# One more pair of batch 2 in cluster order: seven pairs instead of six, with the scatters and waits around it moved

## The chip, the cores and the metric

One core of a Trainium2 chip runs the whole program. The metric is the device time of one execution in microseconds; lower is better. The time before is the median of three runs, 943.9 us (943.89 to 946.26).

## The reference

q, k and v have shape (4, 8, 768, 64): 4 batches, 8 heads, 768 tokens of 64 numbers. Every query and every key is assigned to the one of 16 centroids of its head that it is most similar to, and a query sees only keys of its own cluster:

```python
q_assign = np.argmax(np.einsum('bhsd,hcd->bhsc', q_n, c_n), axis=-1)
k_assign = np.argmax(np.einsum('bhsd,hcd->bhsc', k_n, c_n), axis=-1)
mask = q_assign[:, :, :, None] == k_assign[:, :, None, :]
scores = np.where(mask, scale * np.matmul(q, k.transpose(0, 1, 3, 2)), -1e9)
attn = softmax(scores)                      # over the keys
x = np.matmul(attn, v)                      # -> (4 * 768, 512), heads side by side
h = x @ w_in                                # 512 -> 2048
g = np.maximum(h, 0.0) + alpha * np.minimum(h, 0.0)
return g @ w_out                            # 2048 -> 512
```

## The kernel before, in words

Two heads form a pair, so there are 16 pairs; pairs 0 to 3 belong to batch 0, 4 to 7 to batch 1, 8 to 11 to batch 2 and 12 to 15 to batch 3. The feed-forward network (FFN) of a batch follows its attention and is cut into two halves of 384 tokens.

**Dense pairs.** Attention of a pair is computed in two halves of 384 queries. For each half there are six chunks of 128 keys: `score` (L762) multiplies 384 queries by 128 keys for each of the two heads (L781), ScalarE exponentiates (L799, L802) into one of the E tiles (named E and more), VectorE multiplies by the mask (L822, `mask`), adds the chunks up (L832), turns the sum (L870) and reduces it (L878). TensorE folds that to the denominators (`total`, L891), VectorE takes reciprocals (`invert`, L904) and spreads them (L911); `weigh` multiplies E by v (L936), and `normalise` writes the outcome to the FFN's input xT (L1039).

**Near pairs.** From pair NO = 10 on, the tokens of a pair are first put in the order of their clusters. Then the keys of one chunk can only meet the queries of a `window` (L741) around it: 224, 384, 320, 320, 384 and 224 queries instead of twice 384. Both halves are done in one pass of three steps (`weigh_near`, L956, L969; `normalise_near`, L972, L975). What this costs:
- Ordering: `load` of q and k, `order_features` (two transposes on VectorE, L565), `order_sims` (L573), an argmax (L402 to L410), a transpose (L582) and a scan over the tokens (L587), `order_begins` (two products on TensorE, L599), `order_ranks` and `order_rows` (L607 to L620), `order_clusters` (L637 to L643). The list ORDERS (L1366) holds the step at which each near pair's load is issued; its features follow one step later.
- Scattering: `order_stage` (L652) loads 256 tokens of one head of q, k and v into one of two stage buffers with three DMAs of the SP queue (L659); `order_scatter` (L664) sends 64 tokens of q with 64 of k and v, each to the place that its rank (the tile off) says, by an indirect DMA that GpSimd issues (L673). A pair takes six stages and 24 scatters. They wait in the deque `sorting`; the main loop (L1561 to L1567) takes one per slot, two in the slots of a stage's first step, and none where the pair of the stage before is near. Each such slot begins with `pace` (L646): ScalarE copies one number and GpSimd copies that copy (L649, L650), through one of eight buffers, so that GpSimd doesn't run ahead of the program.
- Loading in order: `order_load` (L679) reads the scattered rows back: the tokens' own numbers into the tile found, q and k in blocks (L694) and v (L703), all on SP. `order_blocks` (L710) and `order_queries` (L716) transpose them on VectorE, one step before the pair's first step.
- Putting back: `to_rows` (L999) transposes the outcomes on TensorE, three tiles at a time and twice; `put_back` (L1005) issues twelve indirect DMAs on GpSimd (L1008), each behind a pace; `fetch_back` (L1013) reads the rows (L1020, SP) and `turn_back` writes them to xT (L1027, VectorE).

**The order of the work** is written out by hand. `steps` (L725) lists the steps: three to a half of a dense pair, three to a near pair. I call three such steps a stage and name it by its first step. In batch 2 the near pairs 10 and 11 come first (steps 48 to 53), then the first halves of pairs 8 and 9 (54 to 59), then their second halves (60 to 65); batch 3 has four near pairs (66 to 77). Each step has five slots (two are taken by the scores in a stage's first step). `begun_at` divides the steps into blocks; at the start of a block `feed_block` (L1423) appends the pieces of one FFN half to the deque `ffn`, and the slots of the block take them at an even rate: 16 pieces `hidden` (L1063, TensorE; L1069 copies, ScalarE; L1055 slopes, VectorE) and 12 pieces `final` (L1081; L1087 or L1089 adds up y). `kept` (L1432) says how many pieces a block leaves to the next one: 12 at the end, 8 before batch 3, 2 at step 60. `later(slots, piece)` (L95) runs a piece some ticks later; a stage has 15 ticks. `prep_at` and `load_at` (L1367 to L1410) place the preparation of each pair by its first step u: features and blocks of q and k (L364), `prep_sims` (L381), `prep_clusters` (L442), keys (L457), and the loads.

The last FFN halves, batch 3's, run in a form with fewer products (`last_pieces`, L1139; L1241 and L1297), with sums formed on VectorE (L1126, L1137, L1220, L1229). Its hidden pieces p1, p5, p2, p6, p3, p7 and the late p4 share banks of PSUM: p4 writes the bank that p7's plus reads.

`check_inverses` (L335) reduces the reciprocals of a batch to their lowest and highest (L340); `inverse` (L329) calls it when the first reciprocal of the next batch is due. The tail (L1579 to L1636) forms a flag from such numbers that says whether a general path has to run; on the inputs here it doesn't.

[...]

## Time and profile before

| | |
|---|---|
| median of three runs | 943.9 us |
| the profiled execution | 944.23 us |
| its span, first to last instruction | 942.5 us |
| TensorE (PE) busy | 924.1 us |
| VectorE (DVE) busy | 663.5 us |
| GpSimd (POOL) busy | 351.2 us |
| ScalarE (ACT) busy | 265.9 us |
| granted TensorE clock | 0.999 |
| scatters (L673), 144 | 1079 ns each |
| returns (L1008), 72 | 1040 ns each |

The page gives busy time by engine and in 40 slices of 23.6 us each, where a digit is the busy share in tenths. Lines of waits read "engine line waited for: us in total, times, longest us". A line of the timeline gives the start, the length of a run of equal instructions, engine, source line, operation, tiles and shape, and how many; an idle stretch ahead of it stands in brackets. A matrix product of 32-bit numbers appears as two records. The table of windows gives busy us of each engine in a stretch:

```profile
core 0: us, PE busy (x) PEld busy (x) DVE busy (x) ACT busy (x) POOL busy (x), PEclk, DMA share, GB/s
445.50:470.10 24.60, 24.60 (x113) 13.43 (x112) 21.50 (x43) 7.47 (x26) 10.77 (x18) 1.00 0.91 151
470.10:508.20 38.10, 36.01 (x151) 17.54 (x150) 29.16 (x59) 7.92 (x22) 14.81 (x25) 1.00 0.22 42
508.20:532.00 23.80, 22.22 (x111) 13.01 (x110) 20.93 (x39) 8.77 (x27) 14.23 (x22) 1.00 0.18 38
532.00:562.30 30.30, 30.30 (x108) 14.65 (x108) 21.07 (x36) 8.28 (x30) 23.93 (x37) 1.00 0.22 55
```

These four stretches are the stages 48, 51, 54 and 57 of the kernel before: near pairs 10 and 11, and the first halves of pairs 8 and 9.

### The profile page before, as it was taken

Reading aid. Unit: us, or ns where it says so; the run is one execution under the profiler, and the core shown is the slowest. Engines: PE = TensorE matmul, PEld = TensorE weight load, DVE = VectorE, ACT = ScalarE, POOL = GpSimd, SP = SyncE. Lnnn points to the kernel's source line nnn. Section 1 sums busy time; section 2 is a strip of 40 time slices with the busy share of each in tenths; the row PEclk is TensorE's granted clock in tenths of the full one; section 3 lists DMA queues with packets and bytes.
Section 4 is the critical chain, followed back from the end, with each engine's and each line's share of the span. In section 5 each row is a group of like instructions: output and inputs, shape, how many; then the busy total and the mean of one; then the engine's idle time right before and its main releaser. Section 6 shows DMA issues by size and latency. Waiting matters only on the chain.

```text
span 942.5 us, 11891 instructions
## 1 busy us (share of the span) xinstructions
PE 924.1 (98%) x3995; PEld 496.5 (53%) x3995; DVE 663.5 (70%) x1247; ACT 265.9 (28%) x658; POOL 351.2 (37%) x529
## 2 busy tenths in 40 slices
PE   8999999999999999999999999999999999999997
PEld 5534444445455454454544545545455555556886
DVE  5797788799679589698995955456888535698100
ACT  5764444323123032331322322223133121221000
POOL 2333222200016576467534686364256670000000
PEclk9999999999999999999999999999999999999999
DMA  8333658039001645165920134333441112000000
GB/s 297 125 127 96 146 130 149 18 59 198 1 6 53 159 87 133 47 120 131 155 52 12 43 80 101 63 67 62 93 75 34 32 37 53 1 0 1 23 23 26
DMA packets 209668, 73.38 MB, mean 78 GB/s; under 512 B 194288, under 2 KB 198080, under 8 KB 209600
## 3 DMA queue, kind: packets, MB, share of 16 engines
q1 hardware_dynamic: 201840, 60.35, 29.2%
q0 software_dynamic: 6912, 11.81, 4.1%
q8 instruction: 33, 0.54, 0.2%
q10 hardware_dynamic: 848, 0.39, 0.2%
q14 instruction: 35, 0.29, 0.1%
HBM read 49.89 MB, written 22.28 MB: 77 GB/s over the span
## 4 chain that ended last, share of the span: by engine, by line
PE 87%; DVE 6%; SPq 2%; DMA 2%; issue 1%; POOL 1%; ACT 1%; ACTq 0%; DVEq 0%; POOLq 0%
PE fps L1081 26%; PE fps L1063 25%; PE vps L936 7%; PE sps L781 7%; PE sps L1297 4%; PE sps L1241 4%; PE fps L781 2%; PE vps L1297 2%; PE vps L1241 2%; PE fps L1297 1%; PE fps L1241 1%; PE sps L790 1%; PE vps L969 1%; PE mps L969 1%; PE mps L381 1%
## 5 line engine op out<-in xcount | busy, mean ns | idle before, releaser
L1063 PE MATMUL fps<-xT,w_in_sb 128*128 128x384 f32 x768 | 257.7, 490 | 0.0
L1081 PE MATMUL fps<-w_out_sb,gT 128*128 128x512 f32 x576 | 254.4, 595 | 1.1 <-DVE gT L1055 1.1
L1063 PEld LDWEIGHTS fps<-xT,w_in_sb 128*128 128x128 f32 x768 | 142.8, 190 | 102.6 <-issue 3.8
L1081 PEld LDWEIGHTS fps<-w_out_sb,gT 128*128 128x128 f32 x576 | 107.5, 190 | 133.4 <-issue 123.0
L673 POOL DMA_INDIRECT scratch<-stage,off x144 | 155.4, 1079 | 49.7 <-issue 25.1
L650 POOL COPY paced<-pace 1x1 f32<-1x1 f32 x196 | 55.5, 283 | 202.3 <-ACT pace L649 201.5
L1069 ACT COPY gT<-fps 128x384 f32<-128x384 f32 x96 | 46.0, 479 | 215.6 <-PE fps L1063 215.6
L1055 DVE SCALAR_TENSOR_TENSOR gT<-gT,alpha 128x384 f32<-128x384 f32 x96 | 61.3, 648 | 50.4 <-ACT gT L1069 50.3
L781 PE MATMUL sps<-qkT 64*128 64x384 f32 (+1 forms) x480 | 88.6, 487 | 0.0
L1008 POOL DMA_INDIRECT back<-rows,found x72 | 74.9, 1040 | 18.2 <-issue 16.1
L802 ACT ACTIVATE E<-sps 128x768 f32<-128x768 f32 (+1 forms) x78 | 57.9, 790 | 59.4 <-PE sps L790 38.8
L781 PEld LDWEIGHTS sps<-qkT 64*128 64x128 f32 x480 | 42.7, 186 | 40.5 <-issue 15.0
L822 DVE SCALAR_TENSOR_TENSOR more<-aq,key,more 128x384 f32<-128x384 bf16 (+2 forms) x120 | 63.0, 584 | 1.2 <-ACT more L799 1.1
L936 PE MATMUL vps<-E,vt 128*64 128x384 f32 x316 | 58.6, 495 | 1.4 <-DVE xT L1039 1.4
L904 DVE RECIPROCAL inverses<-mps 64x12 f32<-64x12 f32 (+1 forms) x44 | 10.9, 248 | 58.5 <-PE mps L891 58.1
L822 DVE SCALAR_TENSOR_TENSOR E<-aq,key,E 128x384 f32<-128x384 bf16 (+2 forms) x96 | 50.2, 577 | 1.9 <-ACT E L799 1.8
L271 POOL TENSOR_TENSOR w_in_sb<-w_in_sb,power 128x512 f32<-128x512 f32 x16 | 25.1, 1573 | 67.8 <-DVE w_in_sb L268 67.8
L832 DVE TENSOR_TENSOR acc<-acc,E 128x768 f32<-128x768 f32 x37 | 35.3, 953 | 14.7 <-ACT E L802 13.6
L271 POOL TENSOR_TENSOR w_out_sb<-w_out_sb,power 128x512 f32<-128x512 f32 x16 | 22.9, 1434 | 57.3 <-DVE w_out_sb L268 57.3
L802 ACT ACTIVATE more<-sps 128x768 f32<-128x768 f32 (+1 forms) x42 | 31.1, 775 | 33.1 <-PE sps L781 32.0
L1087 ACT COPY y<-fps 128x512 f32<-128x512 f32 x18 | 10.6, 586 | 99.1 <-PE fps L1081 99.1
L1089 DVE TENSOR_TENSOR y<-y,fps 128x512 f32<-128x512 f32 x24 | 16.4, 683 | 29.1 <-PE fps L1081 29.1
(283 smaller groups left out, 1167.2 us busy)
## 6 DMA issues: line engine op xcount, KB each, us to landing
raw<-in_moe_w_in_dram SPq DMA_DIRECT2D x16, 512.0 KB
raw<-in_moe_w_out_dram SPq DMA_DIRECT2D x16, 512.0 KB
out_dram<-y SPq DMA_DIRECT2D x21, 256.0 KB
qk<-in_q_dram SPq DMA_DIRECT2D x48, 96.0 KB
qk<-in_k_dram SPq DMA_DIRECT2D x48, 96.0 KB
qk<-scratch SPq DMA_DIRECT2D x48, 96.0 KB
w_in_kept<-w_in_sb SPq DMA_DIRECT2D x8, 512.0 KB
vt<-in_v_dram SPq DMA_DIRECT2D x10, 384.0 KB
```

The source lines that it names most:

```text
L650: nc.gpsimd.tensor_copy(out=sorts["paced"], in_=token)
L673: nc.gpsimd.indirect_dma_start(out=scratch[n][1][h * NX + xx], out_offset=bass.IndirectOffsetOnAxis(ap=ranks[n][:, xx, h:h + 1], axis=0), ...
L781: nc.tensor.matmul(out=bank(ps, h, m), lhsT=qkT[r:r + D, S + c * P:S + (c + 1) * P], rhs=qkT[r:r + D, tokens], start=True, stop=not early_ ...
L802: nc.scalar.activation(out=E[:, :, 0:m], in_=ps[:, :, 0:m], func=AF.Exp, scale=SCALE)
L822: nc.vector.scalar_tensor_tensor(out=e, in0=of, scalar=keys[n][:, NJ + c, h:h + 1], in1=e, op0=ALU.is_equal, op1=ALU.mult)
L936: nc.tensor.matmul(out=po[r:r + D, 0:HS], lhsT=vts[n][:, h, c, :], rhs=e[:, h, :], start=(c == 0), stop=(c == NJ - 1))
L1008: nc.gpsimd.indirect_dma_start(out=to[i], out_offset=bass.IndirectOffsetOnAxis(ap=place[:, h, j:j + 1], axis=0), in_=rows[j // HJ][:, j % ...
L1055: nc.vector.scalar_tensor_tensor(out=gs[f], in0=gs[f], scalar=alpha[:, f:f + 1], in1=gs[f], op0=ALU.mult, op1=ALU.max)
L1063: nc.tensor.matmul(out=ps[:, 0:HS], lhsT=w_in_sb[:, c, f * P:(f + 1) * P], rhs=xTs[b, half][:, c, :], start=(c == 0), stop=(c == NCH - 1))
L1081: nc.tensor.matmul(out=ps[:, 0:DM], lhsT=gs[f][:, i * P:(i + 1) * P], rhs=w_out_sb[:, f, :], start=on and f == f0, stop=off and f == f0 + ...
L1241: nc.tensor.matmul(out=bank[to], lhsT=w_in_form(m, x, cc), rhs=rhs[:, cc, :], start=start and cc == 0, stop=cc == KH - 1, skip_group_check ...
L1297: nc.tensor.matmul(out=bank[to], lhsT=g_form(m, x, t), rhs=w_out_form(n, x), start=start and x == 0, stop=x == NQ - 1, skip_group_check=no ...
```

## The change

- NO becomes 9, so pair 9 is near too: seven pairs are ordered, scattered, computed in one pass and put back. ORDERS has seven entries; the last two loads move from one at step 50 to steps 56 and 59.
- Batch 2 now has the near pairs 9, 10 and 11 (steps 48 to 56) and the two halves of pair 8 (57 to 62), in one block; batch 3 begins at step 63 and the loop ends at step 75 instead of 78. Batch 2's FFN halves are both appended at step 63. The blocks that end at 48 and 63 keep two pieces each.
- `scatters_at` says how many scatters a slot may issue: up to step 50 one more in the first slot of a stage's second and third step (16 in three steps instead of 14), none in steps 51 to 56, one in some slots of 57 to 59 (8), and 20 in three steps from 60 on.
- `order_load` comes three steps ahead of the pair instead of four for pairs 11 and 15 too, and puts the tokens' numbers into the tile off, which held the ranks, instead of a tile found.
- `check_inverses` runs three ticks behind the last reciprocal of a batch instead of ahead of the first of the next; `turn_back` comes seven ticks behind `fetch_back` instead of nine; `prep_blocks` and `prep_sims` move by a slot in some steps; in the last FFN, slopes(f1) moves behind p7's plus, and the pieces are interleaved with the tail's small operations.

```diff
@@ -102,7 +102,7 @@
 
 
     pairs = [(b, hp) for b in range(B) for hp in range(NCH)]
-    NO = WHOLE * NCH - 2
+    NO = WHOLE * NCH - 3
     NP = len(pairs)
     raw_qk, vts = {}, {}
 
@@ -324,12 +324,14 @@
     lowest = const.tile([P, B], FP32, name="lowest")
     highest = const.tile([P, B], FP32, name="highest")
     WORDS = [float((127 + e) * 2 ** 23) for e in (-50, 40)]
-    kept_of = [0]
+    kept_of, inverted = [0], [0] * B
 
     def inverse(n, half):
 
-        if pairs[n][0] > kept_of[0]:
-            check_inverses()
+        b = pairs[n][0]
+        inverted[b] += 1
+        if inverted[b] == 2 * NCH and b < B - 1:
+            later(3, check_inverses)
         return inverses[:, (2 * n + half) % (2 * NCH), :]
 
     def check_inverses():
@@ -679,7 +681,8 @@
     def order_load(n):
         assert len(scattered[n]) == 2 * NX
         whole = scratch.pop(n)[0]
-        found = sorts["order"].tile([P, 2, NJ, 1], I32, name="found")
+        found = ranks[n].rearrange("p x h -> p (x h)")[:, 0:2 * NJ].rearrange(
+            "p (h j d) -> p h j d", h=2, d=1)
         for h in range(2):
             r0 = 2 * h * S
             nc.sync.dma_start(out=found[:, h], in_=whole.bitcast(I32)[
@@ -729,10 +732,10 @@
         begun_at.append(len(steps))
         steps += [(n, None, s) for n in whole for s in range(SB)]
         for half in range(2) if rest else ():
-            if half:
+            if half and not whole:
                 begun_at.append(len(steps))
             steps += [(n, half, s) for n in rest for s in range(SB)]
-            feeds[len(steps)] = b, half
+            feeds[len(steps)] = [(b, 0), (b, 1)] if whole else [(b, half)]
     begun_at.append(len(steps))
     assert NJ == 6 and GROUP == 2
 
@@ -1026,7 +1029,7 @@
             for half in range(2):
                 nc.vector.transpose(out=x_tile(b, half)[:, hp, :],
                                     in_=raw[:, half * HS:(half + 1) * HS])
-        later(4 if n == NP - 1 else 9, turn_back)
+        later(4 if n == NP - 1 else 7, turn_back)
 
     def x_tile(b, half):
         if (b, half) not in xTs:
@@ -1267,10 +1270,10 @@
 
             def p3():
                 plus(g_of(f1, 1), product("e", "S4", x_of(1, 1), False))
-                slopes(f1)
 
             def p7():
                 plus(g_of(f2, 1), product("a", "S3", x_of(1, 0), False))
+                slopes(f1)
                 late.append(p4)
                 if x % 2 == 0 and x:
                     g_sums(x - 2)
@@ -1363,7 +1366,7 @@
     FREE = SLOTS * SB - 3
 
 
-    ORDERS = [26, 29, 35, 38, 41, 50]
+    ORDERS = [26, 29, 35, 38, 41, 56, 59]
     prep_at, load_at = {}, {}
     for (n, half), u in start_of.items():
         def at(step, slot, piece):
@@ -1374,7 +1377,7 @@
             for i in range(2):
                 at(t + 1, FIRST + i, lambda n=n, i=i: order_features(n, i))
             at(t + 2, 2, lambda n=n: order_sims(n))
-            load_at.setdefault(u - (3 if n == NO + 1 else 4), []).append(
+            load_at.setdefault(u - (3 if n in (NO + 1, NO + 2, NP - 1) else 4), []).append(
                 lambda n=n: order_load(n))
             at(u - 4, 0, lambda n=n: prep_clusters(n))
             for i in range(2):
@@ -1395,9 +1398,11 @@
                     at(u - 4, FIRST + g, lambda n=n, g=g: prep_features(n, g))
             else:
                 for w in range(2):
-                    at(u - 7, FIRST + w, lambda n=n, w=w: prep_blocks(n, w))
+                    at(u - 7, FIRST + w + (u - 7 == TOGETHER - 1),
+                       lambda n=n, w=w: prep_blocks(n, w))
             at(u - (3 if n < NCH else 5 if u - 6 < TOGETHER else 6), FIRST,
-               lambda n=n: prep_sims(n))
+               lambda n=n: prep_sims(n)) if u - 6 < 2 * TOGETHER else at(
+                   u - 6, FIRST + 1, lambda n=n: prep_sims(n))
             if n >= NCH:
                 at(u - 4, FIRST if u - 4 < TOGETHER else 0, lambda n=n: prep_clusters(n))
         if n < NCH:
@@ -1412,6 +1417,17 @@
     KEEP = 2
     ffn = deque()
 
+    def scatters_at(v, s, i):
+
+
+        if v < SB:
+            return 1 + (s == 0 or i == 0)
+        if v < 3 * SB:
+            return 0
+        if v < 4 * SB:
+            return int(s == 0 or i % 2 == 0)
+        return 1 + (s == 0 or i % 2 == 0)
+
     def feed(pieces):
         for _ in range(pieces):
             ffn.popleft()()
@@ -1427,12 +1443,13 @@
                 ffn[i] = lambda piece=ffn[i], p=p: (piece(), w_in_sums(p))
             ffn.extend(last_pieces())
             return
-        ffn.extend(ffn_pieces(*feeds[u]))
+        for b, half in feeds[u]:
+            ffn.extend(ffn_pieces(b, half))
 
     def kept(u):
 
 
-        return {NS: 12, begun_at[-2]: 8, begun_at[-3]: 2}.get(block_end(u), 0)
+        return {NS: 12, begun_at[-2]: 2, begun_at[-3]: 2}.get(block_end(u), 0)
 
     def block_end(u):
         return min(x for x in begun_at if x > u)
@@ -1558,7 +1575,7 @@
             places = (block_end(u) - block_start(u)) // SB * FREE
             pieces = len(ffn) - kept(u) + -whole * (places - 1 - at_slot) // places
             todo.popleft()()
-            room = 0 if steps[u - SB][1] is None else 1 + (s == 0)
+            room = scatters_at(u - start_of[NO, None], s, i)
             if room and sorting:
                 pace()
             while sorting and room:
@@ -1577,14 +1594,17 @@
             tick()
         feed(1)
     sum_x(slice(0, 4))
+    feed(2)
     good = const.tile([P, 2], FP32, name="good")
     check_inverses()
+    feed(1)
     nc.vector.tensor_reduce(out=good[:, 0:1], in_=highest, axis=AX.X, op=ALU.max)
     nc.vector.tensor_reduce(out=good[:, 1:2], in_=lowest, axis=AX.X, op=ALU.min)
     nc.vector.tensor_scalar(out=good[:, 0:1], in0=good[:, 0:1], scalar1=WORDS[1],
                             scalar2=None, op0=ALU.is_le)
     nc.vector.tensor_scalar(out=good[:, 1:2], in0=good[:, 1:2], scalar1=WORDS[0],
                             scalar2=good[:, 0:1], op0=ALU.is_ge, op1=ALU.mult)
+    feed(1)
     nc.vector.tensor_reduce(out=good[:, 0:1], in_=alpha, axis=AX.X, op=ALU.max)
     nc.vector.tensor_scalar(out=good[:, 1:2], in0=good[:, 0:1], scalar1=1.0,
                             scalar2=good[:, 1:2], op0=ALU.is_le, op1=ALU.mult)
@@ -1595,7 +1615,7 @@
     for i, p0 in enumerate((P // 2, P // 2 + 1, 0, 1)):
         nc.tensor.matmul(out=ps[0:m, i * NN:(i + 1) * NN], lhsT=ident[:, p0:p0 + m],
                          rhs=sorts["begins"], start=True, stop=True)
-    feed(1)
+    feed(2)
     nc.vector.tensor_copy(out=spans.rearrange("p i n -> p (i n)"), in_=ps[0:m, 0:4 * NN])
     last = const.tile([m, 2], FP32, name="last")
     nc.vector.tensor_tensor(out=last[:, 0:1], in0=ident[0:m, NC - 1:NC],
@@ -1609,6 +1629,7 @@
                                 scalar1=last[:, 0:1], scalar2=last[:, 1:2],
                                 op0=ALU.mult, op1=ALU.add)
 
+    feed(2)
     tiles = const.tile([m, 2, NN], I32, name="tiles")
     nc.vector.tensor_copy(out=tiles[:, 0, :], in_=spans[:, 0, :])
     nc.vector.tensor_scalar(out=tiles[:, 1, :], in0=spans[:, 1, :], scalar1=-1.0,
```

## The prediction

> **What bounds the kernel now.** I read the share of busy time first, then the 40 slices, then what TensorE waited for, and last the timeline of one dense and one near stage. (A stage is three steps, one pair or one pair and half.)
>
> ```profile
> PE 924.1 (98%) x3995; PEld 496.5 (53%) x3995; DVE 663.5 (70%) x1247; ACT 265.9 (28%) x658; POOL 351.2 (37%) x529
> ...
> PE   8999999999999999999999999999999999999997
> ...
> DVE  5797788799679589698995955456888535698100
> ```
>
> TensorE is full in every slice but the first and the last, so work taken from it shortens the kernel one for one, as long as no other engine becomes late. VectorE is the engine to watch: 9 in the slices around 400 to 500 us.
>
> ```profile
> PE mps L599 <- DVE simT L587: 1.6, 1, 1.6
> PE mps L381 <- DVE qk L975: 1.2, 1, 1.2
> ...
> PE mps L969 <- DVE inverses L904: 0.9, 1, 0.9
> ```
>
> These waits (us, times, longest) lie at 516, 478 and 474 us: with 0.9 us late at L1241 and a few before 200 us they are all that TensorE loses after the first 100 us. All three come where VectorE is late, in batch 2's near stages.
>
> ```profile
> 605.59 1.56 PE L781 MATMUL sps<-qkT 64*128 64x384 f32 x8
> ...
> 607.73 0.40 PE L891 MATMUL mps<-part,fold 128*128 128x24 f32 x2
> 608.06 3.45 PE L936 MATMUL vps<-more,vt 128*64 128x384 f32 x20
> ...
> 612.08 0.92 PE L781 MATMUL fps<-qkT 64*128 64x384 f32 x4
> ...
> 614.21 1.12 PE L1081 MATMUL fps<-w_out_sb,gT 128*128 128x512 f32 x2
> ```
>
> One dense half of pair 9, in batch 2: differences of starts give 2.14 us of scores, 0.33 of sums, 4.02 of weighing, 2.13 of scores: 8.62 us.
>
> ```profile
> 696.36 1.29 PE L781 MATMUL sps<-qkT 64*128 64x224 f32 x8
> ...
> 698.12 0.42 PE L891 MATMUL mps<-parts,fold 128*128 128x48 f32 x2
> 698.47 1.79 PE L969 MATMUL vps<-more,vt 128*64 128x384 f32 x16
> ...
> 701.76 0.81 PE L781 MATMUL fps<-qkT 64*128 64x320 f32 x4
> ...
> 703.52 5.43 PE L1063 MATMUL fps<-xT,w_in_sb 128*128 128x384 f32 x16
> 708.78 0.49 PE L999 MATMUL mps<-ident,qk 128*128 128x128 f32 x3
> 709.11 1.13 PE L1063 MATMUL fps<-xT,w_in_sb 128*128 128x384 f32 x3
> ```
>
> A whole near pair: 1.76 + 0.35 + 3.29 + 1.76 = 7.16 us, and 0.33 us for each three transposes of its outcomes.
>
> **What the Trainium skill says.** "Perfetto Trace Analysis", Tensor Engine Instruction: the end of a matmul is estimated by the profiler, so I use starts. The trace agrees that ends mislead: L1063 has a mean of 490 ns, but starts 323 ns apart. "TensorEngine Tiling (Array Packing)", Key Properties: different tiles of the array run in parallel. The trace agrees: eight records of 64 rows (two heads) take 1.39 us to the next group, eight L1063 records of 128 rows 2.6 us; hence I price attention by its own rows, not by columns. "DMA: Bandwidth & Descriptors", SWDGE vs HWDGE: descriptors of DMAs issued by GpSimd are made in software on it, so each scatter costs POOL time (here 1.08 us, against some 0.6 us of SP for one of its DMAs). "VectorE: DVE Perf Modes", The DRAIN you can't avoid: the next operation does not start before the pipe is empty. Here it starts 50 to 90 ns before the end shown of the one ahead; stage 51 (474.13 to 499.85, no idle) took 25.7 us where its mean durations add to 28.5. So I multiply sums of VectorE durations by 0.90.
>
> **The change, part by part.**
>
> 1. Pair 9 from two dense halves to one near pass. TensorE loses 2 x 8.62 = 17.24 us and gets 7.16 + 2 x 0.33 + 0.47 (its order_begins, four records as at 393.03) = 8.29 us. L381 gives way to L573, eight records each. Net 9.0 us off TensorE, all of it on the bound engine: **-9.0**.
>
> 2. VectorE gets less too. Dense pair 9: 24 masks x 0.607, ten adds x 0.951, two turns and two sums (3.8), 4 recip (0.9), two spreads (1.14), two products (1.1), prep 1.9, four query transposes (2.3), argmax 2.6, keys 0.5: about 38.5. Near: masks 6.3, adds 3.5, turns and sums 3.8, recip and spreads 1.8, products 1.1, turn_back 1.1, L710 and L716 3.8, keys 0.5, ordering 11: about 33. The total is no danger; where it lies is.
>
> 3. The stages of batch 2. I added the program's instructions in their new order, at these rows' durations, from one denominator (L891, L904) to the next; VectorE already times 0.90:
> - 42: TensorE 23.2, VectorE 27.0 (one FFN piece went to the next stage, and two are kept); 45: 30.8 and 25.6
> - 48, 51, 54 (near 9, 10, 11): TensorE 23.1, 29.1, 22.3; VectorE 21.5, 24.7, 17.0
> - 57, 60 (pair 8's halves): TensorE 25.4, 28.9; VectorE 25.7, 31.1. In 60 VectorE does 12 masks 7.3, five adds 4.8, ranks of 14 4.6, features and argmax of 15 5.6, blocks and queries of 12 3.8, slopes and y 3.3 and some 5 more: 34.5 before the factor.
> - batch 3: TensorE about 43 a stage, since both halves of batch 2's FFN lie there; VectorE 19 to 27.
> Before, the batch 3 stages were 25 to 28 us and batch 2's last two 43 and 38. So the filler moves behind the stages in which VectorE is loaded. What TensorE needs early: sums (L878) come 5 to 6 us ahead of VectorE's last instruction, and are in time in 45, 60 and 63. L599 needs the scan (L587), near the head of VectorE's stage: in 45 it comes 0.6 us late (4.2 + 5.6 against 9.2), in 60 on time, in 63 about 2 us late (VectorE enters some 3 us behind: 31.1 + 0.5 + 0.5 - 28.9; 3 + 5.1 against 6.3). Cost **+2.6**; zero to six as ends.
>
> 4. Waits that go: check_inverses out of the path of invert (0.9 at 474; the two L340, 0.25 us each, now run behind masks), prep_sims a slot later (1.2 at 478), pair 15's order off step 51 (1.6 at 516). Each of those near stages now has VectorE ahead by 1.6 to 5 us, so nothing else is late in their place: **-3.7**, or 0 if a neighbour takes their place.
>
> 5. slopes(f1) behind p7's plus: TensorE waits 0.9 us once for VectorE, at 860; p4 still waits for that plus. 0; at most -0.9. The interleaved feeds of the tail: TensorE has no wait between 700 and 860 to remove; 0, since the 12 kept pieces (36 us) still cover the return of pair 15, whose L1027 ends at 786 while TensorE asks at 789.5 for it. If that cover goes, each us is lost; its POOL work hangs on the same start, so it doesn't.
>
> 6. found in off's place: its load waited for all scatters anyway; 0 (both bounds a few 0.1 us). turn_back two ticks (3 to 4 us) earlier: the fetches were issued at 523.6 and their packets ended near 528.5, VectorE came at 533.6; VectorE waits 0 to 2 us in stage 54, which has 5 spare; 0.
>
> 7. POOL and SP. 24 scatters and 12 returns more: 24 x 1.08 + 12 x 1.04 + 6 x 0.29 + 9 x 0.28 = 43 us on an engine at 37%; ACT's nine pace copies, 1.7 us of 28%. Per stage of batch 1: 16 x 1.08 + 12 x 0.28 + 4 x 0.29 = 21.8 of 23 to 36 us. Worst is 57 and 60: 12 returns and 8 scatters (27.4 of 25.4), then 6 and 20 with 18 paces and five stage copies (34.3 of 28.9): POOL ends 7 to 8 us late and makes it up in 63 (26.4 of 43). Behind it on SP stand the order loads: pair 13 needs its last scatter at (61, 0), loads at 62, is used at 65; pair 15 (68, 0), 69, 71. A load took 446.8 to about 457, 10 us; so 13 has about 29 us spare, 15 about 18. SP also waits at 59 for the tile of pair 15's raw load, until about 25 us into stage 57; landed 3.5 us into 60, wanted at 6. Eight pace buffers stand for some 16 us before ACT would wait. Cost 0; the other end is a rival.
>
> Sum against the profiled execution (944.2 us, span 942.5): -9.0 + 2.6 - 3.7 = -10.1, so 934.1; the median of the runs is 0.3 below it: **934.0**.
>
> **Rivals.**
> - VectorE takes half back. If in 57 to 63 the overlap is smaller (factor 1: 63.1 us against 54.3) TensorE waits about 4.5 us more than reckoned for L599, L710 and the sums, and the waits of part 4 go on: 944.2 - 9.0 + 4.5, about 939.5. For it: 19.7 of 20 us busy at 460 to 500. Against it: the 25.7 us measured.
> - No change (941 to 946.7): the FFN pieces are too few in batch 2 and waits of about 9 us spread over 42 to 63; or the return of pair 15 (6.6 us of VectorE waiting for that DMA) becomes the end. About 943.
> - Slower: SP's reloads of the two stage buffers stop overlapping with scatters. Exposed, a reload round is 4.3 us of scatters, 2.2 to land, 1.9 of SP, 2.4 of load: 10.8; five a stage are 54 us where stage 60 has 29. POOL would be 25 us late at 63 and about 36 at 66, over the 18 that pair 15 has: L710 then holds VectorE, and TensorE with it, some 16 us: 950. It decides from 18 us of lag. For it: SP waits 218 us in 27 waits for scatters. Against it: POOL waited only 15.7 us in all for reloads in the trace.
>
> **How the numbers follow.** Likeliest (930.5 to 937.5) 0.68, half back (to 941) 0.15, no change 0.09, slower 0.07, still faster 0.01. Within 0.3% of 943.9 (941.1 to 946.7) is about what this measurement can't tell from no change. Range 930 to 941: the low end takes all waits of parts 3 to 5 as gone (-9.0 - 3.7 - 0.9), the high end the first rival. Faster 0.84, same 0.09, slower 0.07.
>
> **What would show it.** L781, L936 and L969 fewer by 9 us of starts; no L340 right ahead of L904; L381 and L969 gone from TensorE's waits, L599 there with 2 to 3 us, around pair 14 or 15. VectorE full from step 57 to 63, TensorE's stages near 25, 29 and 43. Wrong if VectorE's waits for DMA (qk from scratch or back) or POOL's for stage grow over 5 us, or ACT waits at L649.

## The result, and the profile after

The changed kernel took 941.35 us (median of six runs, 940.25 to 941.66) against 943.97 us for the kernel before on the same chip. By these medians it is faster by 2.6 us, a ratio of 0.9972, where 9.9 us were forecast; it lies 0.35 us above the range. The ratio on record is 0.9963 (95% interval 0.9951 to 0.9974): it weighs all runs, and two of the six of the kernel before took 946.3 us. The profiled execution has a span of 939.6 us against 942.5. On two other chips the same kernel was slower than before, by 0.3 and 0.6%; that comes below. One of all executions below (961.63 us, on the sixth chip) fell into a slow state of its chip and is left out of its median.

The lines of the page of the changed kernel that answer to those of before: busy time by engine, and the slices of TensorE and VectorE.

```profile
PE 919.1 (98%) x3963; PEld 495.3 (53%) x3963; DVE 656.2 (70%) x1246; ACT 262.8 (28%) x661; POOL 382.3 (41%) x580
...
PE   8999999999999999999999999999999999999997
...
DVE  5797798799679589598987889754647135598100
```

GpSimd has 31 us more, where 43 were counted. VectorE now stands at 7 to 9 from 400 to some 610 us and at 4 to 6 in the hundred after, as forecast. The slices hide what matters; the list of TensorE's waits (engine, tile and line; who released it; us in all, times, longest) shows it:

```profile
PE fps L1084 <- DVE gT L1058: 2.5, 2, 2.3
...
PE mps L575 <- issue: 1.3, 1, 1.3
PE mps L601 <- DVE simT L589: 1.1, 2, 0.8
PE mps L575 <- ACT rows L1005: 1.1, 1, 1.1
PE mps L972 <- DVE inverses L907: 0.9, 1, 0.9
PE fps L784 <- ACT E L802: 0.7, 1, 0.7
```

(Lines are 2 to 3 higher than before: L975 is L978, L1055 is L1058, L710 is L713.) Of the three waits of before, L381's is gone, the one for L904's reciprocals is still there as L972 on L907, and L599's has two short successors at L601. Two at L575, one of 0.7 us at L784 and one of 2.3 us at L1084 are new.

**The largest one.** The stretch around 490 us in the timeline of the changed kernel, SP's queue first, then VectorE, then TensorE:

```profile
480.40 0.61 SPq L661 DMA_DIRECT2D stage<-in_v_dram  x1
...
482.36 4.61 SPq L697 DMA_DIRECT2D qk<-scratch  x8
...
487.35 0.98 DVE L713 STREAM_TRANSPOSE qkT<-qk 128x768 f32<-128x768 f32 x1 [1.44 <-DMA qk<-scratch]
490.13 0.98 DVE L713 STREAM_TRANSPOSE qkT<-qk 128x768 f32<-128x768 f32 x1 [1.80 <-DMA qk<-scratch]
...
491.45 1.14 DVE L1058 SCALAR_TENSOR_TENSOR gT<-gT,alpha 128x384 f32<-128x384 f32 x2
...
492.11 2.59 PE L1084 MATMUL fps<-w_out_sb,gT 128*128 128x512 f32 x4 [2.29 <-DVE gT L1058]
```

Read it backwards: TensorE waits for gT. VectorE has gT's product (L1058) queued behind L713, pair 11's transposes, and waits 3.2 us there for the DMA, though ScalarE had ended the copy that the first of these products reads at 482.1 us. SP issued that load at 482, behind a reload of the stage buffers, which itself waits for a scatter. Pair 11's last scatter was issued at 414.9 us and had landed by 418.5: what kept the load back is its place in SP's queue.

In the kernel before, the same load of pair 11 goes out at 448, 2.4 us into stage 48, and VectorE comes to it 20 us later, without a wait:

```profile
447.94 5.53 SPq L694 DMA_DIRECT2D qk<-scratch  x8
...
467.48 1.83 DVE L710 STREAM_TRANSPOSE qkT<-qk 128x768 f32<-128x768 f32 x2
```

It was placed three steps ahead of the pair there too, since pair 11 was the second near pair. (The pairs that go from four steps to three are 10 and 15, not 11 and 15 as the list of changes says.) What is new is what stands ahead of it. Pair 11 now begins three steps later, so its load comes behind the reloads for the scatters of stage 48, and these are late:

```profile
465.97 0.97 POOL L675 DMA_INDIRECT scratch<-stage,off  x1 [8.88 <-DMA stage<-in_v_dram]
```

GpSimd waited 8.9 us for a reload that SP issued only at 461.6, behind pair 10's load and pair 8's raw q and k (448 to 461.4). The last two reloads had to wait for the scatters after it, until 473 and 479. So three steps of lead were 20 us before and are 4 us now.

The table of windows (busy us by engine, then PEclk, the granted TensorE clock, third number from the end) shows a second cost:

```profile
492.00:494.00 2.00, 1.89 (x4) 0.68 (x4) 2.00 (x4) 0.00 (x0) 0.00 (x0) 0.84 0.00 0
494.00:496.00 2.00, 2.00 (x7) 1.19 (x8) 0.33 (x1) 0.87 (x3) 0.18 (x1) 0.50 0.00 0
496.00:498.00 2.00, 2.00 (x12) 1.03 (x10) 0.11 (x1) 1.33 (x3) 0.98 (x1) 0.81 0.06 16
```

After the wait the clock falls to half (0.50): over three windows of 2 us, 2 x (0.16 + 0.50 + 0.19) = 1.7 us are lost. The 2.3 us wait cost about 4.

### The profile page after: what moved, and what is told of

It is laid out like the page before. It is cut to its first block, busy times and chain, and to the rows that moved or that the text cites. A ratio compares the mean times of both kernels' runs of the same rounds, so it can differ in the third digit from the quotient of the medians.

```text
span 939.6 us, 11988 instructions
## 1 busy us (share of the span) xinstructions
PE 919.1 (98%) x3963; PEld 495.3 (53%) x3963; DVE 656.2 (70%) x1246; ACT 262.8 (28%) x661; POOL 382.3 (41%) x580
## 4 chain that ended last, share of the span: by engine, by line
PE 82%; DVE 10%; SPq 3%; DMA 1%; issue 1%; POOL 1%; ACT 1%; DVEq 0%; POOLq 0%; ACTq 0%
PE fps L1084 24%; PE fps L1066 22%; PE sps L784 6%; PE vps L939 5%; PE sps L1244 4%; PE sps L1300 4%; PE vps L1244 2%; PE vps L1300 2%; PE fps L784 2%; SPq L697 1%; PE mps L972 1%; PE fps L1300 1%; PE fps L1244 1%; PE vps L972 1%; SPq L127 1%
## 5 line engine op out<-in xcount | busy, mean ns | idle before, releaser
L1084 PE MATMUL fps<-w_out_sb,gT 128*128 128x512 f32 x576 | 254.8, 596 | 2.5 <-DVE gT L1058 2.5
L675 POOL DMA_INDIRECT scratch<-stage,off x168 | 177.9, 1059 | 75.1 <-issue 29.6
L1084 PEld LDWEIGHTS fps<-w_out_sb,gT 128*128 128x128 f32 x576 | 107.4, 190 | 134.8 <-issue 121.4
L1072 ACT COPY gT<-fps 128x384 f32<-128x384 f32 x96 | 46.0, 479 | 236.2 <-PE fps L1066 236.2
L652 POOL COPY paced<-pace 1x1 f32<-1x1 f32 x205 | 51.2, 250 | 139.5 <-ACT pace L651 138.9
L1058 DVE SCALAR_TENSOR_TENSOR gT<-gT,alpha 128x384 f32<-128x384 f32 x96 | 61.2, 647 | 58.7 <-ACT gT L1072 58.5
L1011 POOL DMA_INDIRECT back<-rows,off x84 | 85.7, 1021 | 24.2 <-issue 18.6
L784 PE MATMUL sps<-qkT 64*128 64x384 f32 (+1 forms) x464 | 86.1, 490 | 0.4 <-DVE qkT L713 0.4
L805 ACT ACTIVATE E<-sps 128x768 f32<-128x768 f32 (+1 forms) x76 | 56.3, 786 | 62.6 <-PE sps L793 38.4
L784 PEld LDWEIGHTS sps<-qkT 64*128 64x128 f32 x464 | 41.8, 188 | 39.7 <-issue 14.6
L825 DVE SCALAR_TENSOR_TENSOR more<-aq,key,more 128x384 f32<-128x384 bf16 (+2 forms) x116 | 60.4, 577 | 0.0
L939 PE MATMUL vps<-E,vt 128*64 128x384 f32 x292 | 54.2, 495 | 1.5 <-DVE xT L1042 1.5
L271 POOL TENSOR_TENSOR w_in_sb<-w_in_sb,power 128x512 f32<-128x512 f32 x16 | 25.7, 1612 | 68.6 <-DVE w_in_sb L268 68.6
L825 DVE SCALAR_TENSOR_TENSOR E<-aq,key,E 128x384 f32<-128x384 bf16 (+2 forms) x88 | 45.3, 569 | 0.6 <-ACT E L802 0.6
L907 DVE RECIPROCAL inverses<-mps 64x12 f32<-64x12 f32 (+1 forms) x42 | 10.5, 249 | 48.1 <-PE mps L894 47.9
L835 DVE TENSOR_TENSOR acc<-acc,E 128x768 f32<-128x768 f32 x35 | 33.3, 951 | 14.6 <-ACT E L805 13.6
L805 ACT ACTIVATE more<-sps 128x768 f32<-128x768 f32 (+1 forms) x40 | 29.2, 764 | 12.5 <-PE sps L784 11.6
```

What stands on the lines that cost most here:

```text
L652: nc.gpsimd.tensor_copy(out=sorts["paced"], in_=token)
L675: nc.gpsimd.indirect_dma_start(out=scratch[n][1][h * NX + xx], out_offset=bass.IndirectOffsetOnAxis(ap=ranks[n][:, xx, h:h + 1], axis=0), ...
L784: nc.tensor.matmul(out=bank(ps, h, m), lhsT=qkT[r:r + D, S + c * P:S + (c + 1) * P], rhs=qkT[r:r + D, tokens], start=True, stop=not early_ ...
L805: nc.scalar.activation(out=E[:, :, 0:m], in_=ps[:, :, 0:m], func=AF.Exp, scale=SCALE)
L825: nc.vector.scalar_tensor_tensor(out=e, in0=of, scalar=keys[n][:, NJ + c, h:h + 1], in1=e, op0=ALU.is_equal, op1=ALU.mult)
L939: nc.tensor.matmul(out=po[r:r + D, 0:HS], lhsT=vts[n][:, h, c, :], rhs=e[:, h, :], start=(c == 0), stop=(c == NJ - 1))
```

## Experiments

Theory Q: the missing gain is lost in queues, above all SP's, whose DMAs come a few us too late. Rival V: VectorE is simply full in stages 57 to 63 (the prediction's first rival). Rival M: the single PSUM bank of the mps tiles, into which TensorE writes its small products and from which ScalarE and VectorE read them, is wanted by two at once. "Wait" below is the excess of TensorE's start-to-start times over their usual spacing, 0.1 to 0.4 us more than the idle time in brackets. "First chip" means the one that gave the result. Each block below ran on one chip, every block on another, beside the kernel before; ratios are taken within a chip. The record has no number for the first chip, so it may be one of these five.

### Second chip: four single edits of the changed kernel

Pair 11's load a step earlier:

```diff
-            load_at.setdefault(u - (3 if n in (NO + 1, NO + 2, NP - 1) else 4), []).append(
+            load_at.setdefault(u - (3 if n in (NO + 1, NP - 1) else 4), []).append(
```

> Only pair 11's ordered load is moved, from three steps ahead of the pair to four (step 50 instead of 51), ahead of the last stage-buffer reloads on SP. Theory Q (the queue): VectorE's two waits for qk from scratch (1.4 and 1.8 us at 486 and 488) go, with them TensorE's wait of 2.3 us at 489.7 for gT L1058, and the clock stays at 1.00 afterwards; 3.5 to 4.5 us less than the changed kernel, about 937.2 (0.9929 of the kernel before). Rival V (VectorE is the limit of batch 2 anyway): the wait comes back at the next needs of TensorE (L575, L601 around 525 to 550), and at most 1.5 us are gained: 939.8 or more (0.9956).

Measured: 937.92 us, 0.9929 of before (0.9917 to 0.9941), span 936.1. The load now goes out at 468, VectorE does not wait for it, and the clock stays at 1.00:

```profile
468.27 6.26 SPq L697 DMA_DIRECT2D qk<-scratch  x8
...
486.64 1.83 DVE L713 STREAM_TRANSPOSE qkT<-qk 128x768 f32<-128x768 f32 x2
...
494.00:496.00 2.00, 2.00 (x20) 1.32 (x20) 1.41 (x4) 1.27 (x5) 1.05 (x2) 1.00 0.12 33
```

Nothing comes back elsewhere: TensorE's other waits are those of the changed kernel within 0.4 us each. Theory Q holds for this one. It is worth 0.0034 of ratio against the changed kernel on the first chip (3.2 us; the spans differ by 3.5). The changed kernel itself did not run on this chip; the last of these four edits, which keeps the wait at 490, stands in for it with 0.9964. GpSimd's waits for reloads don't fall with the edit (38.4 us in all, against 28.2 in the changed kernel): what costs time is not that GpSimd is late, but what stands behind it in SP's queue.

Products of order_sims a slot later:

```diff
-            at(t + 2, 2, lambda n=n: order_sims(n))
+            at(t + 2, 3 if n > 13 else 2, lambda n=n: order_sims(n))
```

> The products of order_sims (L575) of pairs 14 and 15 come one slot later, so that their PSUM tile (mps) has been read by the time they are issued. Theory M (the one mps bank): the waits of 1.1 us (533, for L1005) and 1.3 us (559, for L610) go and nothing follows: 2.5 to 2.8 us less than the changed kernel, about 938.7 (0.9945 of before). Rival V (VectorE full in stage 60): the wait at 533, whose reader is ScalarE, goes; the one at 559 comes back at L784 near 575 or at L601 near 585: about 1.2 us less, 940.1 (0.9959).

Measured: 940.09 us, 0.9954 (0.9939 to 0.9968). The wait of 1.2 us at 533 stayed: no FFN piece lay in the added slot, and ScalarE's copy of mps (L1005) still stood behind its L1072. The one at 559 and those at 575 (L713) and 585 went, and one of 2.6 us came at 565:

```profile
568.32 0.25 PE L444 MATMUL mps<-cluster,spread 128*128 128x24 bf16 x4 [2.42 <-DVE simT L404]
```

That is again the mps bank, read late because VectorE was late. So M names the place; the cause, as this trace has it, is VectorE's lateness. The wait at 490 was there with 2.5 us, but in this profile the clock stayed at 1.00, which is worth more than this kernel gains over the changed one. The edit itself is not shown to gain anything.

Pair 14's ordering three steps earlier:

```diff
-    ORDERS = [26, 29, 35, 38, 41, 56, 59]
+    ORDERS = [26, 29, 35, 38, 41, 53, 59]
```

> Pair 14's ordering begins three steps earlier (step 53 instead of 56), so that its features, argmax, scan and ranks leave stage 60 for stage 57, in which VectorE has more room; nothing else is moved by hand. Theory V (VectorE full in stage 60 makes the waits from 552 to 585): the waits at 552, 559, 575 and 577 (about 3 us together) go, the time is 938.3 (0.9940). Theory M (bank and order of pieces): the collision with to_rows moves to the earlier step and keeps its 1.1 us, the one at 559 goes as its partner has left: about 939.8 (0.9956).

Measured: 945.68 us, 1.0010 (1.0002 to 1.0018), the other way. The waits from 552 to 577 did go. Then VectorE, early now, ran into pair 11's return, and TensorE behind it:

```profile
576.98 1.04 DVE L1030 STREAM_TRANSPOSE xT<-qk 128x384 f32<-128x384 f32 x2 [3.92 <-DMA qk<-back]
...
579.98 1.43 PE L784 MATMUL fps<-qkT 64*128 64x320 f32 x2 [5.82 <-DVE y L1092]
```

The last put_back was issued at 570 and the fetch at 572; with turn_back at seven ticks VectorE came at 573. In the changed kernel the fetch goes out at 570, and VectorE, itself late, comes at 577.6. The 5.8 us idle brought 10.2 us of half clock as well.

The end of the kernel as before the change:

```diff
                 plus(g_of(f1, 1), product("e", "S4", x_of(1, 1), False))
+                slopes(f1)
...
                 plus(g_of(f2, 1), product("a", "S3", x_of(1, 0), False))
-                slopes(f1)
...
     sum_x(slice(0, 4))
-    feed(2)
...
     check_inverses()
-    feed(1)
...
-    feed(1)
...
-    feed(2)
+    feed(1)
...
-    feed(2)
```

> The changed kernel with the end of the kernel before: slopes(f1) back in p3, and the FFN pieces between the tail's small operations as they were. In the profiles the stretch from TensorE's last matrix product to the last instruction is 1.3 us shorter after the change. If the interleaved pieces did that, this kernel loses 1.3 us to the changed one: 942.6 (0.9986 of before). If it is how long the last write took to land in that one execution, nothing changes beyond 0.3 us: 941.3 (0.9972), and the stretch varies between profiles whose ends are the same.

Measured: 942.15 us, 0.9964 (0.9950 to 0.9978), as the changed kernel. From the start of TensorE's last product to the last instruction it has 5.3 us, the changed one 5.9, the kernel before 7.1. So the 1.2 us that the end is shorter come neither from the feeds nor from slopes(f1). The trace puts them after SP's last branch: its next instruction follows 2.7 us later before the change, 0.46 us in the changed kernel and in this one.

### Third chip: combinations

All four have pair 11's load at step 50. The first adds order 53 and turn_back at nine ticks; the second also puts pair 10's load at step 47 (the condition is then `n in (NP - 1,)`); the third adds turn_back at nine only; the fourth check_inverses as before only:

```diff
-        later(4 if n == NP - 1 else 7, turn_back)
+        later(4 if n == NP - 1 else 9, turn_back)
```

```diff
-        if inverted[b] == 2 * NCH and b < B - 1:
-            later(3, check_inverses)
+        if b > kept_of[0]:
+            check_inverses()
```

> Pair 11's ordered load at step 50, pair 14's ordering at step 53, and turn_back nine ticks behind fetch_back as before the change (seven was what made VectorE wait 3.9 us for the DMA qk<-back of pair 11 at 573, and TensorE 5.8 us behind it, when only the ordering was moved). Theory V with the return: that wait is gone, and so are those at 552, 559, 575 and 577: about 4 us less than with the load alone, 934 (0.989 of before); span about 931.7. Rival (GpSimd late in stage 60 whatever the tick): VectorE still waits for qk<-back or for the load of pair 12, and the time stays at 937.9 or above (0.993).

> As the one with three edits, and pair 10's ordered load also four steps ahead (47 instead of 48), so that pair 8's raw q and k are issued on SP some 6 us sooner than they were behind that load. Theory Q: VectorE's waits for qk from in_q and in_k at 461 and 464 (0.9 us) go, and with them TensorE's wait for inverses near 465 (1.1 us): 0.7 to 1.1 us less than with three edits, about 933. Rival: the load at 47 holds back the reloads of the stage buffers, the scatters of pairs 12 and 13 end later, and nothing is gained or some us are lost: 934 to 936.

> Pair 11's ordered load at step 50 and turn_back at nine ticks, the ordering of pair 14 left at step 56. Forecast of step 6 of the prediction: nothing, since VectorE does not wait for qk<-back as long as the waits from 533 to 585 are there: 937.9 (0.993 of before), as with the load alone. If seven ticks already cost something there, about 1 us less (936.9).

> Pair 11's ordered load at step 50 and check_inverses as before the change, ahead of the first reciprocal of a new batch. Step 4 of the prediction says that the two L340 (0.25 us each) then stand in TensorE's way: the wait at L972 near 465 grows by 0.4 us, 938.3 (0.9933). Rival: VectorE is held there by the DMA of pair 8's raw q and k anyway, and the two reductions fit into that idle time: no change, 937.9 (0.9929).

Measured: 948.15 us (1.0040, 1.0022 to 1.0057), 949.45 (1.0049, 1.0027 to 1.0072), 945.81 (1.0010, 0.9994 to 1.0026) and 946.37 (1.0015, 1.0001 to 1.0029). All lie 8 to 16 us above what was expected, whatever the edit, so the common part or the chip was at fault. The traces have a kind of wait that no earlier one has: ScalarE and VectorE begin up to 11 us after the shown end of the product they need. I call these late starts. What can still be read: with order 53 and turn_back at nine, the 5.8 us at 574 are 0.9. With the old check_inverses, two L342 stand ahead of L907 and the wait near 465 is 2.0 us against 1.3 with the load alone on the second chip (one profile each), but VectorE waits 1.3 to 1.5 us for pair 8's raw q and k there in both.

### Fourth chip: the same again, with controls

> The changed kernel itself, as a control beside the next three on one chip. If the four kernels of the call before were slow by their own edits, this one is 941.4 (0.9963 to 0.9973 of before) and has no wait of ScalarE or VectorE for a product that TensorE ended over 0.7 us earlier. If the chip made them slow, this one has such waits too and is slower than before or equal.

> The kernel with pair 11's ordered load at step 50 again, as a second control: 0.993 of before if the chip of the call before was the cause of its slow kernels, wherever this chip is not like it; on a chip like it about 1.001.

> The load at step 50, pair 14's ordering at step 53 and turn_back at nine ticks, again. Counted from the first profile without its late signals (2.0 us at 574 and 582, 1.7 us at 555, 1.1 at 466, the rest small) it should be level with the load alone on an undisturbed chip: 0.992 to 0.994. Theory V as first put forecast 0.989.

> The load at step 50 and check_inverses as before the change, again: on an undisturbed chip 0.4 us above the load alone if step 4 of the prediction holds (the wait at L972 near 465 was 1.78 us here against 1.10), nothing if VectorE is held there by its DMA.

Measured: the changed kernel itself 951.05 us, 1.0059 (1.0037 to 1.0080); the load at step 50 949.57, 1.0052 (1.0028 to 1.0075); three edits 950.60, 1.0060 (1.0039 to 1.0080); check_inverses 948.73, 1.0042 (1.0027 to 1.0058). So it was the chip: here the change loses. The load at step 50 has nothing to give back (0.0007): in the changed kernel VectorE, held up by late starts, comes to L713 at 491.6, pair 11's load has landed, and the wait at 490 is not there. The old check_inverses shows nothing either, so the 0.4 us that step 4 has for the two reductions stays unproved. One of the late starts in the changed kernel, TensorE, ScalarE, VectorE:

```profile
444.59 0.81 PE L784 MATMUL fps<-qkT 64*128 64x320 f32 x4
...
448.94 1.55 PE L1084 MATMUL fps<-w_out_sb,gT 128*128 128x512 f32 x3 [2.52 <-ACT E L802]
448.45 0.77 ACT L802 ACTIVATE E<-fps 128x320 f32<-128x320 f32 x2 [7.17 <-remote]
...
448.41 0.56 DVE L1042 TENSOR_TENSOR xT<-vps,rd 128x384 f32<-128x384 f32 x1 [2.42 <-remote]
```

The products in fps end at 445.4 by the trace and those in vps before 444.7; both readers start at 448.4. Counting starts over 0.7 us late after 100 us: 12 here, none in the two kernels on the first chip and none in the four on the second.

### Fifth chip: the kernel before, profiled too

> The kernel before itself, with a profile, beside the changed kernel on one chip: 1.000 of before. On a chip that makes the changed kernel slow (two of the chips so far, 1.006), theory C (late signals come with the dense traffic of the scatters, ordered loads and returns, of which the kernel before has less in batch 2 and 3) expects no or one wait of ScalarE or VectorE over 0.7 us behind a product that TensorE had ended; theory G (the chip delays signals whatever the kernel) expects about as many as in the changed kernel, eight to twelve, hidden by more FFN pieces.

> The changed kernel: 0.996 to 0.997 of before without late signals, 1.006 with them.

> Pair 11's ordered load at step 50: 0.0035 below the changed kernel of the same call if the wait for it is real in every run (0.993 without late signals); with late signals, 1.005 and not below it, since VectorE's wait then lies behind another one.

> Both one-token edits: pair 11's ordered load at step 50 and order_sims of pairs 14 and 15 a slot later. Adding what each did alone (3.3 and 1.2 us less than the changed kernel): 936.8, 0.9917 of before without late signals; if the two gains overlap, 937.9 (0.993). With late signals not below the load alone.

Measured: before 945.06 us, 1.0002 (0.9994 to 1.0011); changed 948.32, 1.0031 (1.0018 to 1.0044); load at step 50 945.68, 1.0001 (0.9985 to 1.0018); both edits 948.30, 1.0043 (1.0023 to 1.0063). The kernel before has three late starts, the changed one six or seven (four of them under 0.9 us). The longest of before:

```profile
756.48 0.56 DVE L975 TENSOR_TENSOR qk<-mps,rd 128x384 f32<-128x384 f32 x1 [3.76 <-PE fps L1063]
```

TensorE goes on with the FFN through it (14 records of L1063 from 752.4); all its waits are those of the first chip, but for one of 0.3 us at 700. So neither theory holds as stated: the late starts also come in the kernel before, but fewer, and this one under cover. In the changed kernel the wait at 490 is there (2.8 us idle, then half clock), and the load at step 50 is worth 0.0030 again (intervals 0.9985 to 1.0018 against 1.0018 to 1.0044); the two edits do not add up.

### Sixth chip: SP's order in stage 60

```diff
-            load_at.setdefault(u - (3 if n in (NO + 1, NO + 2, NP - 1) else 4), []).append(
+            load_at.setdefault(u - (3 if n in (NO + 1, NO + 3, NP - 1) else 4), []).append(
```

> Pair 11's ordered load at step 50, and pair 12's at step 60 instead of 59, where it stood on SP ahead of pair 15's raw q and k (L127). Theory Q in stage 60 too: VectorE no longer waits for qk from in_q at 553 (2.2 us) and from in_k (0.3), so L609 frees the mps bank in time and TensorE's wait at 559 (1.3 us) goes, with most of those at 575 and 585 (0.6 and 0.7): 2 to 2.6 us below the load of pair 11 alone, a ratio 0.0025 lower. Rival V: VectorE is full there by its own work, its wait moves to L713 (the ordered load of pair 12 a step later), and the ratio is level with the load of pair 11 alone.

> The partner on the same chip: pair 11's ordered load at step 50 alone. 0.993 of before without late signals, 1.000 to 1.005 with them; TensorE's waits from 530 to 585 as before (4.6 us).

Measured: 950.94 us, 1.0051 (1.0026 to 1.0075), and 950.53, 1.0061 (1.0041 to 1.0081): level. A reason is seen in the changed kernel's VectorE around 555, against the same place in the first of these two:

```profile
555.25 0.98 DVE L567 STREAM_TRANSPOSE qk<-qk 128x768 f32<-128x768 f32 x1 [2.23 <-DMA qk<-in_q_dram]
```

```profile
554.57 0.95 DVE L567 STREAM_TRANSPOSE qk<-qk 128x768 f32<-128x768 f32 x1
...
579.64 1.04 DVE L1030 STREAM_TRANSPOSE xT<-qk 128x384 f32<-128x384 f32 x2 [3.09 <-DMA qk<-back]
```

The wait of VectorE for pair 15's raw q went, and with it TensorE's at 559 (1.3 us) and for L713 at 575 (0.6). Then pair 11's return was 3.1 us late, and TensorE lost 1.9 us at 586 for L589, plus half clock. Theory Q is right on the cause at 559; removing it uncovers the next DMA, as far as one profile with eleven late starts can show. (Its fetch stands on SP too, issued at 575.)

## Why the prediction was wrong

In us of the profiled execution, as forecast and as measured (the forecast's last line, 934.0, should read 933.8: 934.1 less 0.3):

| step | forecast | measured |
|---|---|---|
| 1: pair 9 near | -9.0 | -7.9 (what the other rows leave) |
| 4: three waits go | -3.7 | -2.8 |
| 3: new waits of stages 42 to 63 | +2.6 | +5.1, and +0.9 at 394 and 401 |
| 7: SP and GpSimd | 0 | +4.2: 2.5 waiting, 1.7 half clock |
| 5: TensorE waits elsewhere (193, 860) | 0 | -1.2 |
| after the last product | 0 | -1.2 |
| sum | -10.1 | -2.9 |

**The step that failed is 7.** It put the cost of SP at 0 after asking only after the loads of pairs 13 and 15. It counted GpSimd's work for batch 1 and for stages 57 and 60, but not when the 16 scatters of stage 48 end, and pair 11's load now stands on SP behind their last reload. That load goes out 19 us into stage 51, VectorE comes to it 4 us later, and by step 7 itself "a load took 446.8 to about 457, 10 us". What the runs show in place of the 0 is 4.2 us: 2.5 of waiting at 490 and 1.7 of half clock after it. One edit, the load a step earlier, gives back 3.2 us by the ratios, of the 7.2 missing. The clock was not foreseen at all. Step 7 also has a part in the row of step 3: the 1.4 us at 559 come from pair 15's raw load, put at 0 there.

Two of the signs that the prediction named for being wrong did come, each by more than its 5 us. VectorE's waits for qk from scratch or back went from 6.6 us to 13.1, GpSimd's for stage from 15.7 to 28.2. Before, then after:

```profile
DVE xT L1027 <- DMA qk<-back: 6.6, 1, 6.6
...
POOL scratch L673 <- DMA stage<-in_v_dram: 15.7, 6, 5.1
```

```profile
DVE xT L1030 <- DMA qk<-back: 9.9, 3, 6.7
DVE qkT L713 <- DMA qk<-scratch: 3.2, 2, 1.8
...
POOL scratch L675 <- DMA stage<-in_v_dram: 27.6, 8, 8.9
...
POOL scratch L675 <- DMA stage<-in_k_dram: 0.6, 2, 0.3
```

**Step 1 held, as far as it can be seen.** After 100 us the starts of L784, L939 and L972 take 8.9 us less than those of L781, L936 and L969 did, with the waits that follow them counted in; 9 were asked for.

**Step 3 had the loads of the engines right and the waits wrong.** Stages 45, 48, 51, 54, 57, 60 and 63 were to take 30.8, 23.1, 29.1, 22.3, 25.4, 28.9 and 43 us of TensorE; they took 30.6, 22.9, 34.2, 22.2, 26.7, 32.9 and 44.0, and the excess in 51, 57 and 60 is the waits. VectorE was busy 19.6, 26.6, 16.8, 24.1 and 30.1 us in stages 48 to 60, against 21.5, 24.7, 17.0, 25.7 and 31.1 forecast; the factor of 0.90 stands. But I looked only for waits for the scan, in stages 45 and 63, 2.6 us in all. Those came to 0.3 and 0.8 us of idle time (L601, stages 60 and 63), and four others stand beside them in stages 57 and 60. At 533 it is two users of the mps bank in neighbouring slots with a ScalarE copy between them, where ScalarE is 28% busy; at 559 the same bank, held because VectorE waited 2.2 us for pair 15's raw q. Step 7 had put its landing 3.5 us into stage 60 and its use at 6: it landed about 9 us in, and VectorE wanted it at 6.7.

**Step 4.** The waits at 478 and 516 went. The one at 474, now near 465, did not, though no L340 is ahead of the reciprocals: VectorE reaches them behind the transposes of pair 8's raw q and k (L366), for which it waits 0.9 us in all. A neighbour did take its place, the case priced there at 0.

**Steps 2, 5 and 6.** VectorE's total fell by 7.3 us (5.5 forecast). slopes(f1): 0.3 us, as good as nothing, as said. turn_back at seven ticks made VectorE wait 2.9 us for a return at 516, and no wait of TensorE there, but it has no slack: order 53 and the sixth chip show it as the next wait. The two last rows of the table, 2.4 us, were not forecast by anything: without this luck the miss would be larger.

**The rivals.** The second had the size, at 943 and with a chance of 0.09: waits of about 9 us spread over stages 42 to 63; they came to 10.2, the clock's loss among them. Its reason, too few FFN pieces in batch 2, was not tested. The first, 939.5, had the wrong reason: VectorE's load was as forecast. Its sum also leaves out the 2.6 us that its 4.5 are said to come on top of; with them it is near 942, and the high end of the range was taken from it. The third had the mechanism: reloads no longer hidden, an order load late behind them, and the transposes (L710, now L713) holding VectorE and with it TensorE. But it put this behind stage 60, at pair 15 and at 16 us, and not behind stage 48, at pair 11 and at 2.5 us. On the two chips with late starts on which the changed kernel ran, the sign itself is against the forecast, by 0.31 and 0.59%, and no case of the prediction had that. A guess that no run tests: TensorE's pieces in batch 2 and 3 now stand where fewer of them cover a late start.

Open: what makes the starts late. Since ends of products are modelled in the trace, the product or its signal may be late. I found no pattern in DMA traffic (the share lies between 0.0 and 1.25 in those stretches); all lie in the time in which GpSimd issues indirect DMAs, which is half of the kernel, and that is no proof.

## What to carry to other kernels

When a change moves a DMA, or puts other DMAs ahead of it, write down for each queue what stands ahead of it, when that is released, and what its reader has queued behind the read: the reader's next instruction for the busiest engine is the one that pays. A lead counted in steps says little: here three steps were 20 us before and 4 us after. A "0" for several transfers on one queue is only as good as the tightest of them, and removing one wait can uncover the next, as with order 53 and on the sixth chip. And test a gain below one per cent on more than one chip: here its sign changed.

## What was not expected of the hardware

- After a wait of TensorE its granted clock can stand at half for 3.4 us, a loss of 1.7 us. It did so after 2.3 us of idle time in the changed kernel on the first chip, after 2.8 on the fifth and after 2.5 with the old end on the second; with other edits three times after 1.9 us (third, fifth and sixth chip; 6.8 us of half clock on the sixth). It did not after the 2.3 us in two kernels of the second chip, nor after 2.5 us in the changed kernel on the fourth. The Trainium skill, "TensorE: Matmul & The Clock Gate", What's actually happening, states half clock after an idle window of about 3.4 us that runs freely; the length of the loss and its coming and going agree with that, but here less than a whole window of idleness was enough.
- The same kernel is 0.9963 of before on one chip and 1.0059 on another, with the kernel before at 944.0 and 945.2 us.
- From SP's last branch to its next instruction pass 2.7 and 2.5 us in the two profiles of the kernel before, and 0.46 us in all 18 of the changed kernel and its edits. The Trainium skill, "Runtime: NRT & Kernel Launch", Instruction fetch mechanics, says that a taken branch may have to fetch its target; that this is it was not tested.
